# Clustered attention with routed experts: who writes the rounded halves of k and q into the operand tiles, and a new plan of the transfers

## The chip, the cores and the metric

One core of a Trainium2 chip runs the whole program. The metric is the device time of one execution in microseconds (us), the median of the runs taken. Engines are named PE (TensorE), ACT (ScalarE), DVE (VectorE), POOL (GpSimd) and SP (SyncE, whose queue starts nearly all transfers).

## What is computed

Attention in which a query sees only the keys of its own cluster, then a layer of eight experts with a limit of 80 tokens each:

```python
q_assign = argmax(einsum('bhsd,hcd->bhsc', q_n, c_n))      # 16 centroids for each head
k_assign = argmax(einsum('bhsd,hcd->bhsc', k_n, c_n))
scores = where(q_assign == k_assign, (q @ k.T) / sqrt(D), -1e9)
x = softmax(scores) @ v                                     # B, H, S, D = 4, 8, 768, 64
x = x.transpose(0, 2, 1, 3).reshape(3072, 512)
expert = argmax(x @ w_gate)                                 # E = 8, the best 80 tokens of each are kept
out[tok] = gate * (relu(x[tok] @ w1[e]) @ w2[e])            # w1: 512x1024, w2: 1024x512
```

## The kernel before

The heads go in 16 pairs (`r` from 0 to 15; four pairs a batch). Attention is the first part of the program, the choice of the tokens and the experts the second.

For each head `g` two operand tiles stand in SBUF, `KAB[g % 6]` and `QAB[g % 6]`, 128 partitions x 2 parts x 768 columns, so six heads have room at a time. A product of full precision is made out of two of lower precision: a number is split into a rounded half `hi` and the rest `lo`. Part 0 of a tile holds `hi` on rows 0 to 63, the cluster's one-hot on rows 64 to 79 and on row 80, for q, the row of the maxima ("shift", `QAB<-row`). Part 1 holds for k `lo` on rows 0 to 63 and `hi` on rows 64 to 127, for q the other way round. The scores of a block are two matmuls, part 1 against part 1 (L470) and part 0 against part 0 (L471). Before that the maxima are found from part 0 alone: matmul `sm` (L433), a reduction on DVE (L435), and once a head is through, a transposition, an ACT copy (L456) and a transfer of 3 KB that puts the row in its place. Exponentials are ACT's (L476), their sums POOL's (L485), the products with v are `av` (L494).

The preparation of a pair runs two pairs ahead of its scores and one ahead of its maxima. `assign` finds the clusters and leaves the one-hots in `oh`. `pair` (L251) then does, in this order: round k on ACT (L269, two instructions), take the rest on POOL (L271), four transfers of k's `hi` into the two heads' tiles (192 KB each as the trace counts them, read and written), two of k's `lo`, four small ones of k's one-hots; then mask q (PE L289, DVE L291), round it on ACT (L295), two transfers of q's `hi` into both parts at once (384 KB each), four small ones of q's one-hots, the rest on POOL (L301), two transfers of q's `lo`. All are started by SP, through the helper `copy` (L79, L80). The maxima of a pair need the keys `("hi", "k")` and `("hi", "q")` (`ready`, L412), its scores `("full", ...)` and the row.

The order of every engine's instructions is written by a planner when the program is made: the class `Flow` plays lanes of `Step`s with fitted durations and due times, and emits each instruction when its turn comes. `CFG` (L20) holds its constants. A transfer is played by `Flow.dma` (L1534): the queue takes 0.6 for each, the engines take them one after another, and the key is ready 1.05 after the end:

```python
for t in times:
    self.queue = max(self.queue, ready) + .6
    self.free["dma"] = max(self.free["dma"], self.queue + .65) + t
return self.free["dma"] + 1.05
```

The plan fixes only the order; on the chip each instruction waits for its operands with semaphores. Eight semaphores are used in turn for SP's transfers, so that a transfer starts only once the eighth before it has landed. Where the planner sees PE idle for longer than 0.25 it puts dummy matmuls (L1424).

Of the kernel before, what the change touches and what calls it, by code (L numbers as in the profile page):

```python
# [18 lines left out]
BASE = 0x3C000000  # L19
CFG = dict(at=dict(sum=-2.92, av=6.36, xT=11.45, lt=5.48, turn=6.25, sm=1.07, exp=-3.24, mx=-0.64), stick=1.99, wait=0.06,  # L20
           idle=0.25, dummy=128, bias=0.67, side=(-1.86, 0.07), prep=(-0.18, 0.32), lead=(-40.37, -29.82, -36.45, -34.77, -18.44),
           zero=(-15.23, 0.59, -7.6, 0.13), start=dict(pe=6.1, act=4.8, dve=7.5, pool=2.5, dma=0.0), warm=48, cold=38.0, lag=0.8,
           hold=dict(dve=(0.08, -0.06), act=(0.67, 0.23), pe=(0.25, 0.02)), nab=6, pps=9, sums=8, xts=4, vs=2, skew=3, raws=4,
           lds=3, keys=1, adds=6, weigh=(8, 5.0, 4.5), slots=(16, 8), native1=(), native2=(0, 1, 2, 3, 4, 5), early=((2, 6),
           185.8), scaled=(), spread=(), mix=dict(ld=-22.86, st=-21.43, hi1=-7.61, lo1=-8.07, hi2=-7.72, lo2=2.21, xg=-34.18,
           xp=-9.37, out=11.74, sc=-9.18, a0=4, a1=2, a2=5, spare=0.3))

# [8 lines left out]
PE, EV = "PE", "EV"  # L36
BOTH = ("dve", "pool")


class Program:  # L40
# [160 lines left out]
    def assign(self, b, p):  # L201
# [33 lines left out]
        nc.tensor.matmul(fi[:, 0:HS], lhsT=self.tie, rhs=es, start=True, stop=True)  # L235
        yield Step("act", .58, also=("dve", .75), needs=[("hi", "q", *divmod(r - 2, self.NP))] if r > 2 else [])
        oh = st["oh", b, p] = w.tile([P, HS], F32R, name="oh", bufs=2)
# [13 lines left out]
    def pair(self, b, p):  # L251

        nc, H, S, D, C, HS, w, copy, flow = self.nc, self.H, self.S, self.D, self.C, self.HS, self.work, self.copy, self.flow
        g0 = b * H + 2 * p
        pos = [g % CFG["nab"] for g in (g0, g0 + 1)]
        free = [("st", (g0 + 2 - CFG["nab"]) * self.NC - 1, 1)] if g0 + 2 > CFG["nab"] else []

        def onehot(n, AB):
            for i, g in enumerate(pos):
                self.onehot(AB[g], self.st["oh", b, p], n == "q", i)  # L260

        yield Step("none", 0.0, needs=[("ld", "k", b, p)])
        t = self.st["k", b, p]
        hi = w.tile([P, S], F32R, name="hi", bufs=2)

        lo = t.bitcast(F32R)
        for f in range(2):
            yield Step("act", .5)
            nc.scalar.copy(hi[:, f * HS:(f + 1) * HS], t[:, f * HS:(f + 1) * HS])  # L269
        yield Step("pool", 1.82, port=BOTH, needs=free + [("sim", b, p)], early=True, dma=[.55] * 4)  # L270
        nc.gpsimd.tensor_tensor(lo, t, hi.bitcast(F32), op=ALU.subtract)  # L271
        for i, g in enumerate(pos):
            r = slice(i * D, (i + 1) * D)
# [7 lines left out]
        yield Step("none", 0.0, needs=[("ld", "q", b, p), ("oh", b, p)])  # L281
# [10 lines left out]
        for f in range(2):  # L292
            fs = slice(f * HS, (f + 1) * HS)
            yield Step("act", .5)
            nc.scalar.copy(hi[:, fs], t[:, fs])  # L295
# [116 lines left out]
    def ready(self, b, h, full):  # L412

        p = h // 2
        if b or p:
            return [("full" if full else "hi", n, b, p) for n in "kq"]
        return [["k0l", "q0l", "full0"], ["k1l", "q1l", "q1h", "k1h", "oh1", ("hi", 1)]][h] if full else [[("hi", 0)], ["k1h", "oh1", ("hi", 1)]][h]
# [19 lines left out]
    def shift(self, b, h):  # L437
# [15 lines left out]
        nc.tensor.transpose(mt, mr, self.ident)  # L453
        yield Step("act", .25, give="misc", key=("shift", g), late=CFG["lag"], dma=[.06], at=NC * g - NC - 4)
        row = w.tile([NC, P], F32R, name="row", bufs=2)
# [50 lines left out]
    def turns(self, r):  # L506

        nc, S, D, HS, NC, w = self.nc, self.S, self.D, self.HS, self.NC, self.work
        b, p = divmod(r, self.NP)
        NJ = HS // P  # L510
        for f in range(2):
            yield Step("pe", .33, needs=[("xT", r, f)], take="misc")
            tp = self.misc([P, NJ, P])
            for j in range(NJ):
                nc.tensor.transpose(tp[:, j, :], self.st["xT", r][:, f, j * P:(j + 1) * P], self.ident)  # L515
            yield Step("act", .48, alt=("dve", .55), give="misc", key=("turn", r, f), dma=[1.1])
# [697 lines left out]
    def prologue(self, flow):  # L1214
# [11 lines left out]
        for p in range(CFG["lds"]):  # L1226
            for n in "kq":
                dma(("ld", n, 0, p), 1.09, self.load, 0, p, n)
            if p == 0:
# [20 lines left out]
        for r in range(CFG["vs"] - 1):  # L1250
            dma(("ldv", r), 1.09, self.load_v, r)
        self.centroids()
# [4 lines left out]
    def stream(self, flow):  # L1257
# [10 lines left out]
        def loads(n):  # L1268

            for r in range(CFG["lds"], R):  # L1270
                yield Step("dma", 1.09, needs=self.taken(n, *divmod(r - CFG["lds"], NP)), key=("ld", n, *divmod(r, NP)))
                self.load(*divmod(r, NP), n)

        def vs():
            for r in range(CFG["vs"] - 1, R):
                yield Step("dma", 1.09, needs=[("av", r - CFG["vs"], NC - 1), ("span", r - CFG["vs"])] if r >= CFG["vs"] else [], key=("ldv", r))
                self.load_v(r)

        def begin(t):
# [19 lines left out]
            if k in (4, 10) and 2 * r + k // 6 < self.NT:  # L1299
                i = 2 * r + k // 6  # L1300
                flow.dma(flow.now, .73)
                nc.sync.dma_start(self.out[i * P:(i + 1) * P, :].rearrange("p (m z) -> p m z", z=P),
# [28 lines left out]
        def weighs():  # L1331
            N1, K1 = self.w1.shape[1] // P, E * self.w1.shape[1] // P
            for n in range(K1):
                u = CFG["weigh"][0] + int(CFG["weigh"][1] * n)
                e, k = divmod(n, N1)
                yield Step("dma", 1.46, key=("wl", n), late=CFG["weigh"][2], needs=[("st", units[u][0] * NC + units[u][1], 0)] + [("wm", n - 1)] * (n > 0), at=u)
                t = self.work.tile([P, self.w1.shape[2]], F32, name="weigh", bufs=1)
# [160 lines left out]
class Flow:  # L1498
# [5 lines left out]
    def __init__(self, free):  # L1504
        self.free, self.end, self.lanes, self.lock = dict(free), {}, [], {}
        self.now, self.kind, self.queue, self.work, self.origin, self.port = 0.0, 0, 0.0, {0: 3000.0, 1: 3100.0}, 0.0, 0.0
        self.idle, self.filled, self.first, self.ahead = None, 0, None, 1e9

    def add(self, *lanes):
# [49 lines left out]
    def run(self):  # L1559
        while True:  # L1560
# [79 lines left out]
            if step.dma:  # L1640
                d = self.dma(start if step.early else done, *step.dma)
                if step.key:
                    self.end[step.key] = d
            self.done = done
# [69 lines left out]
```

## Time and profile before

| | us |
|---|---|
| median of 3 runs | 610.0 (608.13 to 612.93) |
| the profiled execution, its own time | 609.25 |
| its span, first to last instruction | 607.1 |

The profile is of one execution. Busy times are shares of the span; "idle before" is what an engine did not do ahead of a group of instructions, and who ended it. The granted clock of PE has two levels, 1.0 (2.4 GHz) and 0.5 (1.2 GHz). "L433" is a line of the kernel.

### The profile page before, as it was taken

The numbers are of one execution on the slowest core, as the hardware profiler recorded it, in microseconds if no ns is written. First come the engines' busy times: TensorE is split into PE (matmuls) and PEld (weight loads), VectorE is DVE, ScalarE is ACT, GpSimd is POOL, SyncE is SP. The second block draws the span as 40 slices with busy tenths as digits, with TensorE's granted clock in tenths as the row PEclk, the third lists the DMA queues.
The fourth block names the chain that finished last, engine by engine and source line by source line (L and its number), as shares of the span: only waits on it lengthen the run. The fifth ranks groups of instructions, "written<-read, shape, count | busy, mean of one in ns | idle before, by whom it ended". The sixth has DMA issues, their size and how long they took to land.

```text
span 607.1 us, 11292 instructions
## 1 busy us (share of the span) xinstructions
PE 566.0 (93%) x3986; PEld 370.4 (61%) x3986; DVE 416.1 (69%) x815; ACT 331.3 (55%) x704; POOL 393.5 (65%) x226
## 2 busy tenths in 40 slices
PE   7999998998999888989999979999999977899996
PEld 5568565565567465655666556665676457656563
DVE  4866676676577664666876657658777677797872
ACT  7436565565558463664576436555565360554750
POOL 5338696967299694946897928479978121547541
PEclk9558999999999997999999979999999987999999
DMA  7476868786866697688658873855594267799920
GB/s 236 104 178 205 238 180 217 196 235 179 230 178 167 178 239 211 171 231 230 175 152 202 235 237 90 221 134 159 142 375 160 103 216 279 240 391 376 387 100 22
DMA packets 73912, 124.47 MB, mean 205 GB/s; under 512 B 11809, under 2 KB 38977, under 8 KB 73857
## 3 DMA queue, kind: packets, MB, share of 16 engines
q1 hardware_dynamic: 72832, 121.12, 68.0%
q0 software_dynamic: 1024, 2.64, 1.4%
q8 instruction: 31, 0.51, 0.4%
q14 instruction: 25, 0.20, 0.1%
HBM read 70.96 MB, written 13.99 MB: 140 GB/s over the span
## 4 chain that ended last, share of the span: by engine, by line
PE 72%; DMA 11%; issue 5%; SPq 4%; ACT 4%; DVE 3%; POOLq 0%; POOL 0%; ACTq 0%; DVEq 0%
PE av L494 18%; PE sm L433 11%; PE st L470 10%; PE st L471 10%; PE yp L1042 6%; DMA QAB<-row 3%; PE hp L1014 3%; DMA QAB<-oh 3%; SPq L80 3%; DMA out_dram<-room,si 2%; PE misc L532 2%; PE misc L211 1%; PE misc L515 1%; PE misc L289 1%; DMA ldv<-in_v_dram 1%
## 5 line engine op out<-in xcount | busy, mean ns | idle before, releaser
L435 DVE TENSOR_REDUCE mx<-sm 128x1 f32<-128x384 f32 x384 | 203.5, 552 | 87.9 <-PE sm L433 84.6
L485 POOL TENSOR_TENSOR sum<-sum,pp 128x768 f32<-128x768 f32 x122 | 219.5, 1832 | 9.9 <-ACT pp L476 9.5
L476 ACT ACTIVATE pp<-st 128x384 f32<-128x384 f32 x384 | 174.6, 489 | 89.8 <-PE st L471 78.5
L433 PE MATMUL sm<-KAB,QAB 80*128 80x384 f32 x384 | 143.2, 396 | 7.2 <-DMA QAB<-oh 6.2
L494 PE MATMUL av<-pp,ldv 128*64 128x384 f32 x768 | 142.7, 500 | 0.0
L471 PE MATMUL st<-QAB,KAB 81*128 81x384 f32 x384 | 134.0, 349 | 8.2 <-DMA QAB<-row 8.2
L470 PE MATMUL st<-QAB,KAB 128*128 128x384 f32 x384 | 136.7, 356 | 0.0
L485 POOL TENSOR_TENSOR sum<-pp 128x768 f32<-128x768 f32 x32 | 59.4, 1869 | 60.3 <-ACT pp L476 54.2
L433 PEld LDWEIGHTS sm<-KAB,QAB 80*128 80x128 f32 x384 | 74.7, 202 | 30.1 <-issue 12.3
L494 PEld LDWEIGHTS av<-pp,ldv 128*64 128x64 f32 x768 | 48.3, 137 | 63.7 <-issue 61.6
L471 PEld LDWEIGHTS st<-QAB,KAB 81*128 81x128 f32 x384 | 75.7, 197 | 10.0 <-DMA QAB<-row 10.0
L470 PEld LDWEIGHTS st<-QAB,KAB 128*128 128x128 f32 x384 | 75.6, 197 | 5.4 <-issue 4.0
L301 POOL TENSOR_TENSOR ldq<-ldq,hi 128x768 fp32r<-128x768 f32 x15 | 27.6, 1839 | 39.6 <-ACT hi L295 35.7
L1072 POOL DMA_INDIRECT out_dram<-room,si x8 | 25.7, 3212 | 37.8 <-DVE room L1067 28.6
L1340 DVE TENSOR_REDUCE most<-weigh 128x1 f32<-128x1024 f32 x32 | 38.7, 1209 | 3.7 <-DMA weigh<-in_w_dram 3.7
L928 DVE SCALAR_TENSOR_TENSOR w1p<-raw,scales,w1p 128x1024 f16<-128x1024 f32 x29 | 36.1, 1277 | 0.4 <-ACT w1p L917 0.4
L271 POOL TENSOR_TENSOR ldk<-ldk,hi 128x768 fp32r<-128x768 f32 x15 | 27.4, 1828 | 10.6 <-ACT hi L269 7.6
L951 POOL DMA_INDIRECT xg<-xs,gi x8 | 19.9, 2482 | 21.1 <-issue 14.8
L1014 PEld LDWEIGHTS <-w1p 128*128 128x128 f16 x768 | 28.5, 100 | 4.7 <-issue 4.7
L1014 PE MATMUL hp<-xt,w1p 128*128 128x80 f16 x768 | 28.8, 202 | 0.3 <-ACT xt L990 0.3
L917 ACT ACTIVATE w1p<-raw,scales 128x1024 f16<-128x1024 f32 x25 | 27.3, 1143 | 1.3 <-DVE OH L624 1.3
L291 DVE SCALAR_TENSOR_TENSOR ldq<-misc,ldq 128x384 f32<-128x384 f32 x30 | 16.6, 553 | 14.7 <-PE misc L289 13.4
(247 smaller groups left out, 617.9 us busy)
## 6 DMA issues: line engine op xcount, KB each, us to landing
raw<-in_w_dram SPq DMA_DIRECT2D x40, 512.0 KB
weigh<-in_w_dram SPq DMA_DIRECT2D x32, 512.0 KB
KAB<-hi SPq DMA_DIRECT2D x60, 192.0 KB
QAB<-hi SPq DMA_DIRECT2D x30, 384.0 KB
room<-in_w_dram SPq DMA_DIRECT2D x20, 512.0 KB
ldk<-in_kT_dram SPq DMA_DIRECT2D x16, 384.0 KB
ldq<-in_qT_dram SPq DMA_DIRECT2D x16, 384.0 KB
ldv<-in_v_dram SPq DMA_DIRECT2D x16, 384.0 KB
```

The source lines that it names most:

```text
L301: nc.gpsimd.tensor_tensor(lo, t, hi.bitcast(F32), op=ALU.subtract)
L433: nc.tensor.matmul(s, lhsT=qj, rhs=k[0:D + C, 0, f * HS:(f + 1) * HS], start=True, stop=True)
L435: nc.vector.tensor_reduce(mx[:, j, f:f + 1], s, axis=AX.X, op=ALU.max)
L470: nc.tensor.matmul(s, lhsT=k[:, 1, ks], rhs=q[:, 1, qs], start=True, stop=False)
L471: nc.tensor.matmul(s, lhsT=k[0:D + C + 1, 0, ks], rhs=q[0:D + C + 1, 0, qs], start=False, stop=True)
L476: self.nc.scalar.activation(self.st["pp", g, c][:, f], self.st.pop(("s", g, c, f)), AF.Exp, scale=float(self.D) ** -0.5)
L485: eng.tensor_tensor(flat(t), flat(a), flat(self.st["pp", g, c]), op=ALU.add)
L494: nc.tensor.matmul(a[i * D:(i + 1) * D, f, 0:HS], lhsT=v[:, c, i, :], rhs=st["pp", 2 * r + i, c][:, f], start=(c == 0), stop=(c == NC - 1) ...
L928: nc.vector.scalar_tensor_tensor(t[:, 1], raw, s, t[:, 0], op0=ALU.mult, op1=ALU.subtract)
L1014: nc.tensor.matmul(hp[:, f, :], lhsT=wt[:, a, fs], rhs=xt[:, x, k, :], start=(k == 0 and i == 0), stop=(k == K - 1 and i == 2))
L1042: mm = lambda i, l, r, **kw: nc.tensor.matmul(yp[0:Mb, i], lhsT=l, rhs=r, **{"start": False, "stop": False, **kw})
L1340: nc.vector.tensor_reduce(self.most[:, R + n:R + n + 1], t, axis=AX.X, op=ALU.max, apply_absolute_value=True)
```

## The change

Four things are changed in `pair`, and the planner with them.

1. The rounded half of k and of q goes into part 0 of the operand tiles by an ACT copy of 64 partitions x 768 columns from `hi` (`place`), one for each head: four a pair, 60 in all (pair 0 is written by hand elsewhere and stays).
2. The transfers that are left: for k two of `hi` and two of `lo`, for q two of `hi` (now into part 1 alone) and two of `lo`; q's `hi` is sent only after the rest has been taken, beside the `lo`.
3. q's one-hots are sent right after k's, before q is masked and rounded, and have a key of their own, `("ohq", ...)`, which the maxima and the scores need, and the next `oh` tile but one.
4. The planner: a transfer waits for the eighth before it to land; the fixed parts are .55 and .9 in place of .65 and 1.05; durations are CP .85, OH .17, LD 1.3, LV 1.6 and WL 2.2 in place of .55, .1, 1.09, 1.09 and 1.46; a margin `lag` of 1.3 (was .8) is added to the landing of the one-hots and of the shift's row; nearly all due times in `CFG` are new, and so are `skew` (2, was 3: how many steps the second head of the first pair lags), the last number of `weigh` (1.5, was 4.5), `slots` (15 and 9, were 16 and 8), `a1` (4, was 2) and `a2` (2, was 5).

```diff
-    self.queue = max(self.queue, ready) + .6
-    self.free["dma"] = max(self.free["dma"], self.queue + .65) + t
-return self.free["dma"] + 1.05
+    self.queue = max(self.queue, ready, self.landed.pop(0)) + .6
+    self.free["dma"] = max(self.free["dma"], self.queue + .55) + t
+    self.landed.append(self.free["dma"] + .9)
+return self.free["dma"] + .9
@@ pair
+        def place(AB, hi):
+            for i, g in enumerate(pos):
+                yield Step("act", .87, needs=free)
+                nc.scalar.copy(AB[g][0:D, 0, :], hi[i * D:(i + 1) * D, :])
...
-        yield Step("pool", 1.82, port=BOTH, needs=free + [("sim", b, p)], early=True, dma=[.55] * 4)
+        yield from halves(hi, t)
+        yield Step("pool", 1.82, port=BOTH, needs=free + [("sim", b, p)], early=True, dma=[CP] * 2)
         nc.gpsimd.tensor_tensor(lo, t, hi.bitcast(F32), op=ALU.subtract)
         for i, g in enumerate(pos):
-            copy(self.KAB[g][0:D, 0, :], hi[r, :])
-            copy(self.KAB[g][D:2 * D, 1, :], hi[r, :])
-        yield Step("none", 0.0, key=("full", "k", b, p), dma=[.55] * 2)
+            copy(self.KAB[g][D:2 * D, 1, :], hi[i * D:(i + 1) * D, :])
+        yield from place(self.KAB, hi)
+        yield Step("none", 0.0, key=("full", "k", b, p), dma=[CP] * 2)
...
-        yield Step("none", 0.0, needs=[("oh", b, p)], key=("hi", "k", b, p), dma=[.1] * 4)
+        yield Step("none", 0.0, needs=[("oh", b, p)], key=("hi", "k", b, p), late=CFG["lag"], dma=[OH] * 4)
         onehot("k", self.KAB)
+        yield Step("none", 0.0, needs=[("ld", "q", b, p), ("oh", b, p)], key=("ohq", b, p), late=CFG["lag"], dma=[OH] * 4)
+        onehot("q", self.QAB)
...
-        yield Step("none", 0.0, key=("hi", "q", b, p), dma=[1.09] * 2 + [.1] * 4)
-        for i, g in enumerate(pos):
-            copy(self.QAB[g][0:D], hi[i * D:(i + 1) * D].unsqueeze(1).broadcast_to([D, 2, S]))
-        onehot("q", self.QAB)
+        yield from halves(hi, t)
+        yield from place(self.QAB, hi)
+        yield Step("none", 0.0, key=("hi", "q", b, p))
         yield Step("pool", 1.82, port=BOTH)
         nc.gpsimd.tensor_tensor(lo, t, hi.bitcast(F32), op=ALU.subtract)
-        yield Step("none", 0.0, key=("full", "q", b, p), dma=[.55] * 2)
+        yield Step("none", 0.0, key=("full", "q", b, p), dma=[CP] * 4)
+        for i, g in enumerate(pos):
+            copy(self.QAB[g][0:D, 1, :], hi[i * D:(i + 1) * D, :])
         for i, g in enumerate(pos):
             copy(self.QAB[g][D:2 * D, 1, :], lo[i * D:(i + 1) * D, :])
```

## Rows read from the trace of the kernel before

**Rows 1.** The page: the span, PE and its granted clock by slices, the chain
```profile
span 607.1 us, 11292 instructions
...
PE 566.0 (93%) x3986; PEld 370.4 (61%) x3986; DVE 416.1 (69%) x815; ACT 331.3 (55%) x704; POOL 393.5 (65%) x226
...
PEclk9558999999999997999999979999999987999999
...
PE av L494 18%; PE sm L433 11%; PE st L470 10%; PE st L471 10%; PE yp L1042 6%; DMA QAB<-row 3%; PE hp L1014 3%; DMA QAB<-oh 3%; SPq L80 3%; DMA out_dram<-room,si 2%; PE misc L532 2%; PE misc L211 1%; PE misc L515 1%; PE misc L289 1%; DMA ldv<-in_v_dram 1%
```

**Rows 2.** Busy time of each engine (us, instructions), clock and DMA by stretch
```profile
15.00:50.00 35.00, 33.23 (x122) 23.91 (x123) 25.17 (x57) 15.37 (x34) 14.51 (x8) 0.51 0.65 172
50.00:487.00 437.00, 416.29 (x2436) 267.48 (x2434) 297.91 (x588) 252.08 (x580) 321.03 (x178) 0.98 0.70 193
227.00:234.00 7.00, 4.90 (x15) 2.66 (x15) 3.17 (x5) 1.94 (x5) 4.88 (x3) 0.51 0.66 175
356.00:364.00 8.00, 6.59 (x21) 6.04 (x21) 3.04 (x7) 3.88 (x8) 2.23 (x2) 0.57 0.72 223
487.00:519.00 32.00, 23.05 (x357) 20.28 (x356) 23.09 (x75) 11.25 (x17) 6.25 (x13) 0.84 0.71 254
519.00:600.00 81.00, 80.72 (x966) 49.98 (x964) 62.84 (x67) 42.15 (x57) 42.27 (x13) 1.00 0.76 274
```
The columns: the stretch, its length, busy PE, PE's weight loads, DVE, ACT, POOL, granted clock, share of the DMA engines, GB/s.

**Rows 3.** Waits of PE: who waited for whom, us in total, times, longest
```profile
PE st L471 <- DMA QAB<-row: 8.2, 5, 3.3
PE sm L433 <- DMA QAB<-oh: 6.2, 4, 3.5
```

**Rows 4.** The chain from 217 to 230 us: start, us, what
```profile
217.68 0.93 ACT hi L295 x2
...
220.42 0.70 SPq L80
...
221.17 0.63 SPq L80
...
221.85 7.16 DMA QAB<-oh
...
229.10 0.66 PE sm L433
```

**Rows 5.** The chain elsewhere: two rows and a one-hot
```profile
143.58 5.46 DMA QAB<-row
...
197.42 2.00 DMA QAB<-oh
...
354.11 3.25 DMA QAB<-row
```

**Rows 6.** Groups by line: shapes, count, busy us, mean ns, idle before, releasers
```profile
L476 ACT ACTIVATE pp<-st 128x384 f32<-128x384 f32 x384 | 174.6, 489 | 89.8 <-PE st L471 78.5 <-PE av L494 3.2 <-POOL sum L485 2.3
...
L295 ACT CAST hi<-ldq 128x384 fp32r<-128x384 f32 x30 | 14.3, 511 | 1.2 <-DVE ldq L291 0.9
...
L456 ACT CAST row<-misc 6x128 fp32r<-6x128 f32 x32 | 8.1, 254 | 24.9 <-PE misc L453 23.3 <-DMA raw<-in_w_dram 1.3
...
L938 ACT CAST w2p<-room 128x1024 fp32r<-128x1024 f32 x4 | 4.2, 1043 | 2.6 <-PE hp L1014 2.6
...
L403 DVE CAST QAB<-ldq 64x768 fp32r<-64x768 f32 x1 | 0.5, 543 | 0.0
...
L470 PEld LDWEIGHTS st<-QAB,KAB 128*128 128x128 f32 x384 | 75.6, 197 | 5.4 <-issue 4.0 <-ACT x L519 0.6 <-ACT pp L476 0.3
```

**Rows 7.** Issues of transfers: what, engine, operation, count, KB each
```profile
KAB<-hi SPq DMA_DIRECT2D x60, 192.0 KB
QAB<-hi SPq DMA_DIRECT2D x30, 384.0 KB
...
QAB<-ldq SPq DMA_DIRECT2D x30, 192.0 KB
```

More of the change, by code (lines that the diff above doesn't have):

```diff
@@ L19 @@
 BASE = 0x3C000000
[L20 to L26, printed above, removed]
+CFG = dict(at=dict(sum=-3.46, av=6.5, xT=9.63, lt=2.62, turn=6.52, sm=2.41, exp=-3.44, mx=-1.76), stick=1.61, wait=0.05,
+           idle=0.25, dummy=128, bias=0.18, side=(-1.52, -0.17), prep=(-0.75, 0.12), lead=(-39.66, -31.86, -37.47, -37.48,
+           -18.17), zero=(-15.24, 0.53, -11.87, 0.25), start=dict(pe=6.1, act=4.8, dve=7.5, pool=2.5, dma=0.0), warm=48,
+           cold=38.0, lag=1.3, hold=dict(dve=(0.08, -0.02), act=(0.7, 0.04), pe=(0.26, 0.04)), nab=6, pps=9, sums=8, xts=4, vs=2,
+           skew=2, raws=4, lds=3, keys=1, adds=6, weigh=(8, 5.0, 1.5), slots=(15, 9), native1=(), native2=(0, 1, 2, 3, 4, 5),
+           early=((2, 6), 185.8), scaled=(), spread=(), mix=dict(ld=-22.93, st=-22.34, hi1=-3.09, lo1=-20.55, hi2=4.02, lo2=2.78,
+           xg=-34.32, xp=-10.34, out=9.27, sc=-5.2, a0=4, a1=4, a2=2, spare=0.54))
 SWITCH = {(0, 1): .01, (1, 0): .01, (0, 2): .108, (1, 2): .108, (2, 0): .16, (2, 1): .196, (0, 0): 0.0, (1, 1): 0.0, (2, 2): 0.0}
@@ L37 @@
 BOTH = ("dve", "pool")
+CP, OH, LD, LV, WL = .85, .17, 1.3, 1.6, 2.2
 class Program:
@@ L260, in onehot, with halves @@
                 self.onehot(AB[g], self.st["oh", b, p], n == "q", i)
+        def halves(hi, t):
+            for f in range(2):
+                fs = slice(f * HS, (f + 1) * HS)
+                yield Step("act", .5)
+                nc.scalar.copy(hi[:, fs], t[:, fs])
+        def place(AB, hi):
+            for i, g in enumerate(pos):
+                yield Step("act", .87, needs=free)
+                nc.scalar.copy(AB[g][0:D, 0, :], hi[i * D:(i + 1) * D, :])
         yield Step("none", 0.0, needs=[("ld", "k", b, p)])
@@ L291, in pair @@
             nc.vector.scalar_tensor_tensor(t[:, fs], mask, 1.0 / BIG, t[:, fs], op0=ALU.mult, op1=ALU.mult)
[L292 to L295, printed above, removed]
-        yield Step("none", 0.0, key=("hi", "q", b, p), dma=[1.09] * 2 + [.1] * 4)
-        for i, g in enumerate(pos):
-            copy(self.QAB[g][0:D], hi[i * D:(i + 1) * D].unsqueeze(1).broadcast_to([D, 2, S]))
-        onehot("q", self.QAB)
+        yield from halves(hi, t)
+        yield from place(self.QAB, hi)
+        yield Step("none", 0.0, key=("hi", "q", b, p))
         yield Step("pool", 1.82, port=BOTH)
         nc.gpsimd.tensor_tensor(lo, t, hi.bitcast(F32), op=ALU.subtract)
-        yield Step("none", 0.0, key=("full", "q", b, p), dma=[.55] * 2)
+        yield Step("none", 0.0, key=("full", "q", b, p), dma=[CP] * 4)
+        for i, g in enumerate(pos):
+            copy(self.QAB[g][0:D, 1, :], hi[i * D:(i + 1) * D, :])
         for i, g in enumerate(pos):
@@ L415, in ready @@
         if b or p:
-            return [("full" if full else "hi", n, b, p) for n in "kq"]
+            return [("full" if full else "hi", n, b, p) for n in "kq"] + [("ohq", b, p)]
         return [["k0l", "q0l", "full0"], ["k1l", "q1l", "q1h", "k1h", "oh1", ("hi", 1)]][h] if full else [[("hi", 0)], ["k1h", "oh1", ("hi", 1)]][h]
@@ L453, in shift @@
         nc.tensor.transpose(mt, mr, self.ident)
-        yield Step("act", .25, give="misc", key=("shift", g), late=CFG["lag"], dma=[.06], at=NC * g - NC - 4)
+        yield Step("act", .4, give="misc", key=("shift", g), late=CFG["lag"], dma=[0.0], at=NC * g - NC - 4)
         row = w.tile([NC, P], F32R, name="row", bufs=2)
@@ L515, in turns @@
                 nc.tensor.transpose(tp[:, j, :], self.st["xT", r][:, f, j * P:(j + 1) * P], self.ident)
-            yield Step("act", .48, alt=("dve", .55), give="misc", key=("turn", r, f), dma=[1.1])
+            yield Step("act", .48, alt=("dve", .55), give="misc", key=("turn", r, f), dma=[.6])
             x = self.con.tile([P, NJ, P], F32, name="x", bufs=3)
@@ L1227, in prologue @@
             for n in "kq":
-                dma(("ld", n, 0, p), 1.09, self.load, 0, p, n)
+                dma(("ld", n, 0, p), LD, self.load, 0, p, n)
             if p == 0:
@@ L1250, in prologue @@
         for r in range(CFG["vs"] - 1):
-            dma(("ldv", r), 1.09, self.load_v, r)
+            dma(("ldv", r), LD, self.load_v, r)
         self.centroids()
@@ L1270, in loads @@
             for r in range(CFG["lds"], R):
-                yield Step("dma", 1.09, needs=self.taken(n, *divmod(r - CFG["lds"], NP)), key=("ld", n, *divmod(r, NP)))
+                yield Step("dma", LD, needs=self.taken(n, *divmod(r - CFG["lds"], NP)), key=("ld", n, *divmod(r, NP)))
                 self.load(*divmod(r, NP), n)
@@ L1275, in vs @@
             for r in range(CFG["vs"] - 1, R):
-                yield Step("dma", 1.09, needs=[("av", r - CFG["vs"], NC - 1), ("span", r - CFG["vs"])] if r >= CFG["vs"] else [], key=("ldv", r))
+                yield Step("dma", LV, needs=[("av", r - CFG["vs"], NC - 1), ("span", r - CFG["vs"])] if r >= CFG["vs"] else [], key=("ldv", r))
                 self.load_v(r)
@@ L1300, in begin @@
                 i = 2 * r + k // 6
-                flow.dma(flow.now, .73)
+                flow.dma(flow.now, .7)
                 nc.sync.dma_start(self.out[i * P:(i + 1) * P, :].rearrange("p (m z) -> p m z", z=P),
@@ L1335, in weighs @@
                 e, k = divmod(n, N1)
-                yield Step("dma", 1.46, key=("wl", n), late=CFG["weigh"][2], needs=[("st", units[u][0] * NC + units[u][1], 0)] + [("wm", n - 1)] * (n > 0), at=u)
+                yield Step("dma", WL, key=("wl", n), late=CFG["weigh"][2], needs=[("st", units[u][0] * NC + units[u][1], 0)] + [("wm", n - 1)] * (n > 0), at=u)
                 t = self.work.tile([P, self.w1.shape[2]], F32, name="weigh", bufs=1)
@@ L1507, in __init__ @@
         self.idle, self.filled, self.first, self.ahead = None, 0, None, 1e9
+        self.landed = [0.0] * 8
     def add(self, *lanes):
@@ L1642, in run @@
                 if step.key:
-                    self.end[step.key] = d
+                    self.end[step.key] = d + step.late
             self.done = done
```

7 lines of the change are left out of this document (1 added, 6 removed).

## The prediction

> **What bounds the kernel now.** I read the page first: PE is busy for 93% of the span, DVE 69%, POOL 65%, ACT 55% [rows 1]. So PE sets the time, and a change is worth what it gives back of PE's idle time or of its slow clock, or what it adds to them. The slices of the granted clock show where the clock is not full: near the start, in two single slices in the middle, and around the choice of the tokens [rows 1].
>
> The view by stretches prices this [rows 2]. From 50 to 487 us attention runs, and PE is busy for 416.29 of 437 us: 20.7 us idle. From 519 to 600 us the experts run, with PE busy for 80.72 of 81 us at full clock: no planner's constant can shorten that without taking matmuls away, and the change takes none. Between the two, 32 us go to the choice of the tokens, which isn't edited. The start, 15 to 50 us, has PE busy for 33.23 of 35 us at a clock of 0.51.
>
> The view of PE's waits tells who makes the idle time in attention: scores wait 8.2 us in five places for the row of the maxima, maxima wait 6.2 us in four places for q's one-hots, each up to 3.5 us [rows 3]. Together 14.4 of the 20.7 us are waits for a small transfer. The two longest are followed by a stretch at the lower clock: after the wait that ended at 229.1 us [rows 4] the stretch 227 to 234 has 0.51, and around the wait that ended at 357.4 (354.11 and 3.25 on) [rows 5] the stretch 356 to 364 has 0.57 [rows 2]. PE did 4.90 and 6.59 us of busy time there; at the upper clock the first takes half, some 2.5 us less, and of the second what lies at the lower level, some 6.2 us, takes 3.1 less. So the waits and what follows them cost 14.4 + 5.6 = 20.0 us, the most that attention between 50 and 487 us can give back by this cause.
>
> The chain of waits shows why the one-hots are late [rows 4]. q is rounded at 217.68 to 218.61. SP starts the two large transfers of q's half at 220.42 and 221.17, the one-hots are behind them at 221.85, and these 24 KB land 7.16 us later. PE takes the next maximum at 229.10, 10.5 us after q was rounded. A one-hot that stood less behind landed in 2.00 us [rows 5]. The row of the next head comes out of the maxima, so a pair whose maxima start late sends its rows late: the same cause stands behind a part of the 8.2 us. The rest of that part is the queue: the row at 143.58 took 5.46 us [rows 5].
>
> **The change part by part.**
>
> *One-hots of q sent early.* They need only `oh`, which is ready before q is masked, so they now land while PE masks q and ACT rounds it. Instead of two transfers of 384 KB and four of 24 KB behind the rounding there are two ACT copies. From the end of the rounding to the first maximum this takes two copies of about 0.87 us, 1.7 us, and with an exponential of 0.489 us [rows 6] ahead of each 2.7 us, in place of 10.5 [rows 4]. So in the worst place maxima may start some 8 us earlier than they did, more than the longest wait of 3.5 us [rows 3]. All of the 6.2 us should go, and the 2.5 us of slow clock behind the longest: 8.7 us.
>
> *Rows.* They follow the maxima, and are due earlier by as much; but q's last transfers are now four of 192 KB where two were [rows 7], and a row that falls behind them waits for two more. The planner now counts with eight in flight and a margin of 1.3. I take two thirds of the 8.2 + 3.1 us, 7.3 us; the bounds are nothing and all 11.3.
>
> *Bytes.* For a pair, twelve units of 192 KB (four of k's half, two of its rest, two double ones of q's half, two of its rest [rows 7]) become eight; over 15 pairs 11.5 MB fewer, at 193 GB/s [rows 2] some 60 us of the queue's time, and two transfers fewer in 18. This is off PE's path except where a wait above names it; I count nothing beyond the rows and the one-hots.
>
> *ACT's copies.* No row has 64 partitions x 768 on ACT. Bounds: a cast of 128 columns takes 254 ns, of 384 columns 511, of 1024 columns 1043 [rows 6]. From the first two 1.0 ns a column gives 511 + 384 = 895 ns; from the last two 0.83 ns a column gives 830 ns. I take 870 ns, 60 times: 52 us. ACT is busy for 252.08 of the 437 us of attention [rows 2], and would stand at some 70%. What hides it is ACT's own idle time, 89.8 us before exponentials, 78.5 of it waiting for PE [rows 6]. What it can cost is a late exponential: three banks hold the scores, and PE stops if ACT is three behind. The 60 casts of 511 ns that ACT already does for the same halves have left 0.3 us of wait on exponentials in the group of 384 weight loads [rows 6]. So the low bound is nothing, and the high one the full 52 us, as if no exponential could be moved aside. I take 2 us, next to the low end, as the copies are the same sort of work as those casts.
>
> *The planner's other constants.* They move no work between engines in attention. The new times for loads (LD, LV, WL) put transfers at other places of SP's queue; `skew` and the due times change the order of PE's first 50 us. I count nothing for them and give the start a case of its own below. In the experts, `slots`, `a1`, `a2` and the due times move ACT's and DVE's splitting of weights, hidden behind a PE that is full [rows 2]; without that cover each microsecond of a late weight would be one of time. The choice of the tokens has the same chain of small steps.
>
> *Sum.* Against the profiled execution's own 609.25 us (span 607.1 [rows 1]): less 8.7, less 7.3, plus 2, is 595.2; it lies within 1 us of the median, 610.0. I forecast 595.0 us.
>
> **The rivals.**
>
> *A. The rows stay late.* The maxima come earlier, but the row stands behind four transfers of q in place of two, and the margin only moves it in the plan. For it: the row of 3 KB took 5.46 us in a place where the queue was full [rows 5], and the row is the larger of the two waits [rows 3]. Against it: a third of the bytes is gone. Then only 8.7 us come back: 609.25 - 8.7 + 2 = 602.5 us.
>
> *B. The waits come back elsewhere.* PE is busy for 95% of attention, the plan is new from end to end, and each place in which PE's order and the data don't meet costs again. If they cost the same 20 us as now, the change does not do what it says, and the time stays at 609 us. For it: the planner of before plays the same keys and rows, and 14.4 us of waits for them are in the trace. Against it: the planner now counts the eight transfers.
>
> *C. ACT becomes late (the other side).* 60 copies of 0.87 us stand between exponentials. If each costs PE half its length, 26 us, the time is 609.25 - 16 + 26 = 619 us. It decides at 0.38 us a copy: from there on the 16 us are eaten up and 1% more is lost. For it: six hundred ACT instructions of attention [rows 2] wait for each other in order, and a copy is nearly twice as long as an exponential. Against it: the 0.3 us [rows 6]. The Trainium skill, "ScalarE: Activation LUTs", section "Rules for kernel authors", speaks against this placing: it gives simple elementwise work (it lists relu, max, min, add and mul) to VectorE rather than ScalarE, since VectorE is faster for each element. The trace bears out the price: the one such cast on DVE, 64x768, took 543 ns [rows 6]; but DVE has 297.91 us of 437 to do and ACT 252.08 [rows 2].
>
> *D. The start gets its full clock earlier.* From 15 to 50 us PE works at 0.51 [rows 2]. If pair 1's maxima, ready sooner, fill PE so that the clock rises 14 us earlier, 7 us more come back: 588 us. Nothing in the rows says that it must.
>
> **How the numbers follow.** The forecast (both waits go, 591 to 599) has 0.50, A 0.18, B 0.14, C 0.11, D 0.07. One per cent, 6 us, is about what a measurement here can tell from no change: faster is below 603.9, slower above 616.1. The forecast and D are faster; A lies near the bound, and I give it two thirds to faster, one third to within; B is within; C mostly slower. That makes 0.70 faster, 0.19 within, 0.11 slower. The range reaches from D's neighbourhood, 587, over A to the edge of B, 609; what is left out is C, half of B and the lower part of D, some 2 in 10.
>
> **What would show it.** Right: in the profile after, PE's waits for QAB<-oh are gone and those for QAB<-row are below 3 us; the granted clock stays at 1.0 from 50 us to the end of attention, which ends about 473 us in place of 487; the copies of 64x768 on ACT take 0.83 to 0.90 us; the part from the end of attention to the end stays within 2 us of its 120 us. Wrong: waits of PE's scores for ACT's exponentials of several us (C); rows that land in 5 us (A); waits of like sum for other transfers or engines (B); a clock that is full well before 50 us (D). Also wrong, if the experts' stretch moved by more than 3 us.

## The result, and the profile after

The kernel after takes 586.86 us in the median of four runs (585.59 to 588.72), the kernel before 609.84 beside it: a ratio of 0.962, with a 95% interval of 0.957 to 0.967. The forecast was 595.0 with a range from 587.0 to 609.0. The direction was right; the gain is 23 us in place of 15, and the time lies 0.14 us below the range.

The profiled execution of after took 587.6 us, of before 609.25. First the page of after, the lines that answer to [rows 1]:

```profile
span 585.8 us, 11321 instructions
...
PE 562.4 (96%) x4015; PEld 368.3 (63%) x4015; DVE 430.3 (73%) x850; ACT 359.6 (61%) x729; POOL 381.9 (65%) x226
...
PEclk9559999999999999999999999999999877999999
...
PE av L501 24%; PE sm L440 14%; PE st L477 12%; PE st L478 11%; DMA out_dram<-room,si 6%; PE misc L539 2%; PE misc L522 2%; PE misc L212 2%; PE misc L299 1%; POOL xg L958 1%; DMA raw<-in_w_dram 1%; DMA ldv<-in_v_dram 1%; PE misc L220 1%; PE misc L460 1%; PE sm L539 1%
```

The two slow slices in the middle are gone, and no transfer of QAB is left among the lines of the chain that the page shows. Lines of `pair` and below have moved: L433 is now L440, L470 and L471 are L477 and L478, L494 is L501.

The stretches of after, to be held against [rows 2] (stretch, length, busy PE, weight loads, DVE, ACT, POOL, granted clock, DMA share, GB/s). Attention now ends at 459, the choice of the tokens at 495, the experts' matmuls at 581:

```profile
15.00:50.00 35.00, 34.18 (x139) 21.84 (x140) 26.67 (x61) 19.86 (x39) 12.88 (x8) 0.61 0.53 139
50.00:459.00 409.00, 407.28 (x2426) 263.85 (x2424) 306.35 (x613) 278.30 (x605) 323.71 (x179) 1.00 0.64 180
459.00:495.00 36.00, 25.03 (x375) 21.65 (x372) 27.14 (x81) 15.24 (x20) 7.03 (x13) 0.78 0.70 250
495.00:581.00 86.00, 85.29 (x977) 53.35 (x975) 61.65 (x69) 35.50 (x49) 28.99 (x13) 0.97 0.68 247
```

In attention PE stands idle for 1.7 us, where it was 20.7, and its clock is full throughout. In the two later parts the reader sees the opposite: the choice takes some 36 us in place of 32, at a clock of 0.78 in place of 0.84, and the experts' stretch has 0.97 in place of 1.00.

Put together from the trace's marks (the start of the last `av` matmul of the first and of the last pair, the start of the first `hp`, the end of the last `yp`):

| part | before | after | difference |
|---|---|---|---|
| start, to the last av of pair 0 | 71.3 | 70.3 | -1.0 |
| attention, from there to the last av | 410.1 | 383.2 | -26.9 |
| choice, from there to the first hp | 38.2 | 41.6 | +3.4 |
| experts, first hp to last yp | 82.4 | 85.5 | +3.1 |
| end | 5.2 | 5.2 | 0 |

The sum is -21.4 us, and the spans differ by 21.3. These are traces of one execution of each kernel. The attention of after came out at 383.2 us in three traces that share its plan there; before was traced once.

The waits of PE in after, to be held against [rows 3]. The long ones that are left stand in the choice and just ahead of the first expert. Of the 1.7 us in attention, 0.4 us is a wait for a row, and none is for a one-hot:

```profile
PE q L708 <- DVE dug L654: 2.7, 1, 2.7
PE tp L992 <- ACT room L971: 2.4, 1, 2.4
PE q L708 <- DVE alive L751: 2.0, 1, 2.0
...
PE st L478 <- DMA QAB<-row: 0.4, 1, 0.4
```

And the place that answers to [rows 4], the same pair, by the timeline (start, us, engine, line, operation). The second pair of L267 casts ends at 210.62, the two ACT copies at 212.95; the one-hots were started at 208.49:

```profile
208.49 2.44 SPq L81 DMA_DIRECT2D QAB<-oh  x4
...
209.53 0.52 ACT L267 CAST hi<-ldq 128x384 fp32r<-128x384 f32 x1
...
210.11 0.51 ACT L267 CAST hi<-ldq 128x384 fp32r<-128x384 f32 x1
...
210.90 0.81 ACT L272 CAST QAB<-hi 64x768 fp32r<-64x768 f32 x1
...
212.12 0.83 ACT L272 CAST QAB<-hi 64x768 fp32r<-64x768 f32 x1
...
215.72 0.38 PE L440 MATMUL sm<-KAB,QAB 80*128 80x384 f32 x1
```

The pair's first maximum is the one at 215.72, 5.1 us after q was rounded, where it was 10.5; the `sm` rows before it belong to the pair ahead. PE did not wait for it: the plan put it there.

### The profile page after: what moved, and what is told of

Same layout as the page of the kernel before. It is cut to its first block, busy times and chain, and to the rows that moved or that the text cites. A ratio compares the mean times of both kernels' runs of the same rounds, so it can differ in the third digit from the quotient of the medians.

```text
span 585.8 us, 11321 instructions
## 1 busy us (share of the span) xinstructions
PE 562.4 (96%) x4015; PEld 368.3 (63%) x4015; DVE 430.3 (73%) x850; ACT 359.6 (61%) x729; POOL 381.9 (65%) x226
## 4 chain that ended last, share of the span: by engine, by line
PE 73%; issue 11%; DMA 9%; DVE 3%; POOL 1%; SPq 1%; ACT 1%; POOLq 0%; DVEq 0%
PE av L501 24%; PE sm L440 14%; PE st L477 12%; PE st L478 11%; DMA out_dram<-room,si 6%; PE misc L539 2%; PE misc L522 2%; PE misc L212 2%; PE misc L299 1%; POOL xg L958 1%; DMA raw<-in_w_dram 1%; DMA ldv<-in_v_dram 1%; PE misc L220 1%; PE misc L460 1%; PE sm L539 1%
## 5 line engine op out<-in xcount | busy, mean ns | idle before, releaser
L442 DVE TENSOR_REDUCE mx<-sm 128x1 f32<-128x384 f32 x384 | 201.1, 550 | 57.1 <-PE sm L440 54.1
L501 PE MATMUL av<-pp,ldv 128*64 128x384 f32 x768 | 143.7, 498 | 0.1
L440 PE MATMUL sm<-KAB,QAB 80*128 80x384 f32 x384 | 141.3, 396 | 0.6 <-DVE mx L442 0.3
L477 PE MATMUL st<-QAB,KAB 128*128 128x384 f32 x384 | 134.5, 350 | 0.0
L478 PE MATMUL st<-QAB,KAB 81*128 81x384 f32 x384 | 130.4, 340 | 0.4 <-DMA QAB<-row 0.4
L440 PEld LDWEIGHTS sm<-KAB,QAB 80*128 80x128 f32 x384 | 72.1, 198 | 28.3 <-issue 11.8
L501 PEld LDWEIGHTS av<-pp,ldv 128*64 128x64 f32 x768 | 47.1, 136 | 61.0 <-issue 58.4
L477 PEld LDWEIGHTS st<-QAB,KAB 128*128 128x128 f32 x384 | 73.3, 191 | 6.8 <-issue 4.8
L478 PEld LDWEIGHTS st<-QAB,KAB 81*128 81x128 f32 x384 | 73.4, 191 | 0.7 <-DMA QAB<-row 0.7
L1079 POOL DMA_INDIRECT out_dram<-room,si x8 | 21.2, 2648 | 40.6 <-DVE room L1074 36.1
L958 POOL DMA_INDIRECT xg<-xs,gi x8 | 11.4, 1429 | 35.4 <-DVE room L975 20.8
L1021 PE MATMUL hp<-xt,w1p 128*128 128x80 f16 x768 | 31.3, 208 | 0.3 <-DVE xt L999 0.2
L1030 ACT ACTIVATE hh<-hp 128x320 f32<-128x320 f32 (+1 forms) x16 | 7.0, 437 | 35.4 <-PE hp L1021 30.5
L935 DVE SCALAR_TENSOR_TENSOR w1p<-raw,scales,w1p 128x1024 f16<-128x1024 f32 x22 | 27.5, 1277 | 0.4 <-ACT w1p L924 0.4
L272 ACT CAST KAB<-hi 64x768 fp32r<-64x768 f32 x30 | 24.8, 828 | 0.4
```

The lines of the kernel that those rows point to most:

```text
L440: nc.tensor.matmul(s, lhsT=qj, rhs=k[0:D + C, 0, f * HS:(f + 1) * HS], start=True, stop=True)
L442: nc.vector.tensor_reduce(mx[:, j, f:f + 1], s, axis=AX.X, op=ALU.max)
L477: nc.tensor.matmul(s, lhsT=k[:, 1, ks], rhs=q[:, 1, qs], start=True, stop=False)
L478: nc.tensor.matmul(s, lhsT=k[0:D + C + 1, 0, ks], rhs=q[0:D + C + 1, 0, qs], start=False, stop=True)
L501: nc.tensor.matmul(a[i * D:(i + 1) * D, f, 0:HS], lhsT=v[:, c, i, :], rhs=st["pp", 2 * r + i, c][:, f], start=(c == 0), stop=(c == NC - 1) ...
L935: nc.vector.scalar_tensor_tensor(t[:, 1], raw, s, t[:, 0], op0=ALU.mult, op1=ALU.subtract)
```

## The experiments

The runs were made in groups, and each ratio is to the kernel before in the same group, on the same chip. There before took 613.58 us (the first four rows under after, up to "one-hots late"), 609.42 us (the two with "same plan", the one moved the other way and the last row) or 611.27 us (the other four), so ratios are a better guide than medians across the groups. "Attention" is the stretch from the last `av` of pair 0 to the last one, as in the table above, with the time PE stood idle in it and the time it had the lower clock.

| kernel | median us | ratio, 95% interval | attention | idle | lower clock |
|---|---|---|---|---|---|
| before | 609.84 | 1 | 410.1 | 20.4 | 13.7 |
| after | 586.86 | 0.962, 0.957 to 0.967 | 383.2 | 1.7 | 0 |
| new pair, old plan | 599.67 | 0.975, 0.970 to 0.981 | 400.5 | 10.0 | 6.8 |
| old pair, new plan | 599.76 | 0.980, 0.973 to 0.986 | 393.2 | 6.3 | 0 |
| halves by SP | 602.13 | 0.978, 0.972 to 0.984 | 399.1 | 8.6 | 10.2 |
| one-hots late | 602.01 | 0.979, 0.974 to 0.984 | 401.0 | 4.9 | 10.2 |
| halves by SP, same plan | 622.55 | 1.021, 1.014 to 1.029 | 417.1 | 21.2 | 23.9 |
| one-hots late, same plan | 610.29 | 1.004, 1.000 to 1.008 | 401.5 | 13.6 | 10.2 |
| ACT copies twice | 601.62 | 0.983, 0.977 to 0.989 | 397.5 | 11.8 | 0 |
| after, constants moved | 602.00 | 0.984, 0.977 to 0.991 | 388.3 | 3.5 | 0 |
| after, moved the other way | 592.64 | 0.973, 0.968 to 0.978 | 386.6 | 3.0 | 3.4 |
| before, constants moved | 606.62 | 0.993, 0.988 to 0.998 | 403.4 | 16.2 | 3.4 |
| more dummies | 585.33 | 0.956, 0.951 to 0.961 | 383.2 | 1.7 | 0 |
| more dummies, old experts' constants | 587.98 | 0.967, 0.962 to 0.972 | 383.2 | 1.7 | 0 |

**The two halves of the change, crossed.** The theory was that the shorter preparation gives the gain; the rival, that the new plan does.

```diff
# new pair, old plan: after, with the planner's constants and transfer model of before
-CP, OH, LD, LV, WL = .85, .17, 1.3, 1.6, 2.2
+CP, OH, LD, LV, WL = .55, .1, 1.09, 1.09, 1.46
...
-    self.queue = max(self.queue, ready, self.landed.pop(0)) + .6
+    self.queue = max(self.queue, ready) + .6
# old pair, new plan: after, with pair() and ready() of before, costed by the fitted times
-        yield Step("none", 0.0, key=("hi", "q", b, p), dma=[1.09] * 2 + [.1] * 4)
+        yield Step("none", 0.0, key=("hi", "q", b, p), late=CFG["lag"], dma=[2 * CP] * 2 + [OH] * 4)
```

> The edits of the pair's preparation (ACT copies, one-hots early, q's half later) under the planner of before: its constants, its transfer model and its due times. Theory (the shorter preparation gives the gain): most of the 23 us stay, 588 to 597 us, and PE's waits for QAB<-oh are gone. Rival (the new plan gives the gain): 603 to 610 us, with waits for QAB<-row or others of over 8 us.

> The preparation of before (all halves by SP's transfers, q's one-hots behind them) under the planner of after: new constants, eight transfers in flight, margins, the fitted 0.85 for each 192 KB. Theory (the shorter preparation gives the gain): 602 to 612 us, with waits of PE for QAB<-oh of 5 us or more. Rival (the plan gives the gain): 586 to 594 us.

Neither theory stands alone: each half by itself gives 2 to 2.5%. In attention the two add up: 410.1 becomes 400.5 by the preparation and 393.2 by the plan, 26.5 us in sum, and both together give 26.9. How close that is means little, as neighbouring plans, further below, move attention by 3 to 7 us. The waits of PE for the new pair under the old plan:

```profile
PE st L478 <- DMA QAB<-row: 4.3, 3, 2.4
...
PE misc L220 <- ACT row L463: 2.1, 6, 0.3
PE misc L299 <- ACT row L463: 1.9, 6, 0.3
```

and of the old pair under the new plan:

```profile
PE st L472 <- DMA QAB<-row: 2.2, 3, 1.1
...
PE misc L212 <- ACT row L457: 0.3, 1, 0.3
```

The waits for q's one-hots are gone in both: the preparation sends them early, or the plan, which now counts with late landings, puts PE's instructions in another order. Waits for the row are halved by the one and cut to a quarter by the other. The rows on L220, L299 and L212 are of a kind that the prediction had not looked at: after the row's transposition the next matmul into the same PSUM bank waits for ACT's copy of the row, 0.3 us at a time. The old plan has it with either preparation, the new one hardly: all places in attention together, 4.2 us in before, 4.0 for the new pair under the old plan, 0.5 for the old pair under the new plan, 0.3 in after. The lines of before:

```profile
PE misc L289 <- ACT row L456: 2.5, 7, 0.4
...
PE misc L219 <- ACT row L456: 1.4, 4, 0.3
```

Among the changes of the planner is one that the list in "The change" leaves out: its step for that copy is 0.4 us in place of 0.25. It is the likely reason, but it was not changed by itself.

**Each part of the preparation undone, with a new plan.**

```diff
# halves by SP (the keys ("hi", "k") and ("hi", "q") need "placed" too)
+            yield Step("none", 0.0, needs=free, key=("placed", id(AB), b, p), dma=[CP] * 2)
             for i, g in enumerate(pos):
-                yield Step("act", .87, needs=free)
-                nc.scalar.copy(AB[g][0:D, 0, :], hi[i * D:(i + 1) * D, :])
+                copy(AB[g][0:D, 0, :], hi[i * D:(i + 1) * D, :])
...
# one-hots late: from behind k's to behind the rounding and the ACT copies of q
-        yield Step("none", 0.0, needs=[("ld", "q", b, p), ("oh", b, p)], key=("ohq", b, p), late=CFG["lag"], dma=[OH] * 4)
-        onehot("q", self.QAB)
...
+        yield Step("none", 0.0, key=("ohq", b, p), late=CFG["lag"], dma=[OH] * 4)
+        onehot("q", self.QAB)
```

> The kernel after, but the halves go into part 0 by SP's transfers in place of ACT's copies (four more transfers of 192 KB a pair); one-hots stay early, all constants stay. If early one-hots are what matters, 586 to 592 us; if ACT's copies matter (fewer bytes, no landing behind the rounding), 595 to 605 us, with PE waiting for QAB<-hi.

> The kernel after, but q's one-hots are sent behind the rounding of q again (four transfers of 24 KB with nothing large right ahead of them); ACT's copies stay. If early one-hots are what matters, 595 to 605 us with waits for QAB<-oh; if the two large transfers ahead of them were the trouble, 586 to 591 us.

Both cost the same against after, 1.7 and 1.8% by the ratios, and by the traces all of it in attention (16 and 18 us longer; in the second the part ahead of it is 3.8 us shorter). But hardly any of it is a wait for a transfer: PE waits 1.6 us for QAB<-hi in the first and for no one-hot in the second. More idle time and the lower clock make 12 of the 16 us and 8 of the 18; the rest is PE busy for longer and was not taken apart. A planner that counts with the later data makes another plan, with constants that had been chosen for something else. So these two runs could not tell a part's worth from that of the plan.

**The same, with the plan held still.** Here PE, DVE and POOL keep after's order to the instruction, ACT too but for the copies taken out; the planner counts as if nothing were changed.

```diff
# one-hots late, same plan: only the place of the call moves
         yield Step("none", 0.0, needs=[("ld", "q", b, p), ("oh", b, p)], key=("ohq", b, p), late=CFG["lag"], dma=[OH] * 4)
-        onehot("q", self.QAB)
...
         yield Step("none", 0.0, key=("hi", "q", b, p))
+        onehot("q", self.QAB)
...
# halves by SP, same plan
                 yield Step("act", .87, needs=free)
-                nc.scalar.copy(AB[g][0:D, 0, :], hi[i * D:(i + 1) * D, :])
+                copy(AB[g][0:D, 0, :], hi[i * D:(i + 1) * D, :])
```

> The plan of after kept instruction for instruction on PE, ACT, DVE and POOL; only SP sends q's one-hots four instructions behind the rounding of q instead of right after k's. Theory (the early one-hots carry a part of the gain by themselves): 592 to 602 us, PE's waits for QAB<-oh 5 us or more. Rival (with nothing large ahead of them they land in time anyway): 586 to 590 us.

> The plan of after kept on PE, DVE and POOL, and on ACT but for the 60 copies; the halves go into part 0 by four transfers of 192 KB a pair from SP at the same places. Theory (ACT's copies spare the landing behind the rounding): 597 to 612 us, with waits of PE for QAB<-hi. Rival (the 52 us of ACT work cost what the transfers would): 584 to 590 us.

Each undoes the whole gain or more in the time of the program, further than either theory had it. In attention, where the gain was 26.9 us, the late one-hots cost 18.3 us and the halves by SP 33.9. PE's waits with the one-hots late:

```profile
PE sm L440 <- DMA QAB<-oh: 6.4, 5, 1.6
PE sm L440 <- issue: 4.6, 3, 2.6
```

with the halves by SP:

```profile
PE sm L440 <- DMA QAB<-hi: 8.1, 4, 4.0
PE sm L440 <- issue: 5.1, 3, 2.1
...
PE st L478 <- DMA QAB<-row: 2.3, 3, 1.0
```

"issue" is time in which PE waited for nothing that the profile shows. The idle time is back (13.6 and 21.2 us) and with it the lower clock (10.2 and 23.9 us). The early one-hots and the ACT copies are thus both needed by this plan. The late one-hots have nothing large right ahead of them and still make PE wait, so the rival of that run is out. What each is worth in a plan made for its absence, these two runs don't tell.

**What ACT has left.**

```diff
                 nc.scalar.copy(AB[g][0:D, 0, :], hi[i * D:(i + 1) * D, :])
+                nc.scalar.copy(AB[g][0:D, 0, :], hi[i * D:(i + 1) * D, :])
```

> The kernel after with each of the 60 ACT copies of 64x768 issued twice, in the same plan (the planner is not told): 50 us more of ACT work. Theory (ACT's idle time hides the copies): at most 4 us more than after, PE's waits for exponentials below 3 us. Rival (ACT is near its bound): 10 us or more, with PE waiting for ACT pp.

The rival was right about the second 50 us. ACT's groups, and then a wait of PE:

```profile
L484 ACT ACTIVATE pp<-st 128x384 f32<-128x384 f32 x384 | 173.6, 487 | 49.7 <-PE st L479 44.4 <-DMA KAB<-hi 0.5
...
L273 ACT CAST KAB<-hi 64x768 fp32r<-64x768 f32 x30 | 25.0, 832 | 0.9
L273 ACT CAST QAB<-hi 64x768 fp32r<-64x768 f32 x30 | 25.0, 832 | 1.0
```

```profile
PE st L478 <- ACT pp L484: 6.9, 11, 0.8
```

Attention grows by 14.3 us (383.2 to 397.5), 0.24 us for each copy added, 29% of its length. In after itself PE has no wait for exponentials to show: the first 50 us, which the plan counts, cost none there, and the next 50, which it does not count, do. Whether a plan that counts them too fares better was not tried.

**Neighbouring plans.** Four of the planner's constants were moved by 0.05 to 0.1. The work is the same but for some dummy matmuls and, in two of the three, some copies (ten in the first) that change between ACT and DVE; what differs is the order.

```diff
# the four entries of CFG alone
# after, constants moved (the other way: 6.6, -3.49, 1.56, 0.13)
-av=6.5,  exp=-3.44,  stick=1.61,  bias=0.18
+av=6.4,  exp=-3.39,  stick=1.66,  bias=0.23
# before, constants moved
-av=6.36,  exp=-3.24,  stick=1.99,  bias=0.67
+av=6.26,  exp=-3.19,  stick=2.04,  bias=0.72
```

> The kernel after with four of the planner's constants moved a little (av 6.5 to 6.4, exp -3.44 to -3.39, stick 1.61 to 1.66, bias 0.18 to 0.23); the work is the same, the order a neighbouring one. Theory (the shorter preparation and the fitted model carry the gain, any near plan keeps it): 585 to 591 us where before is at 610. Rival (a good part of the gain is this one plan, and is lost with any move): 596 to 603 us, with waits or a slow clock in attention.

> The kernel before with the same moves (av 6.36 to 6.26, exp -3.24 to -3.19, stick 1.99 to 2.04, bias 0.67 to 0.72). It tells how far a plan of before moves by itself: if the plans of before are chosen points too, 612 to 622 us; if not, 606 to 613 us.

> The kernel after with the four constants moved the other way (av 6.6, exp -3.49, stick 1.56, bias 0.13): a second neighbouring plan. If a neighbouring plan keeps the gain in attention, its attention takes 380 to 392 us from the first pair to the last (after 383.2, the first neighbour 388.3, before 410.1), whatever choice and experts do; if the gain sits in this one plan, 398 us or more. The whole: 588 to 604 us.

After's neighbours are slower than after by 13 and 6 us by the ratios, before's neighbour is some 4 us faster than before. The first neighbour's time lies where its rival had it, but not for the rival's reason: in attention the neighbours keep most of the gain, 388.3 and 386.6 us against 383.2 for after's, 403.4 against 410.1 for before's. So of the 26.9 us between the two kernels there, about 21 are left between the means (386.0 for the three plans with the new edits, 406.8 for the two with the old) and 16 between the neighbours alone; the rest is this pair of plans. The waits go with the edits and not with the draw: before's neighbour waits 5.5 us for rows and 3.3 us for q's one-hots, after's neighbours 0.6 us at most for a row and not at all for q's one-hots. The slow neighbour lost 9.5 us in the experts, most of it at one place, a matmul that waited 6.3 us for an ACT instruction:

```profile
PE yp L1049 <- ACT hh L1030: 6.6, 2, 6.3
```

**The later parts.** In after, one long run of 73 dummy matmuls stands between the choice and the first expert. PE's rows (start, us, what, idle before it):

```profile
486.39 4.24 PE L1431 MATMUL tot<-one 128*128 128x128 f16 x73
493.08 0.45 PE L992 MATMUL tp<-K,room 80*128 80x80 f16 x4 [2.45 <-ACT room L971]
494.10 0.45 PE L992 MATMUL tp<-K,room 80*128 80x80 f16 x4 [0.57 <-DVE room L975]
...
495.12 5.73 PE L1021 MATMUL hp<-xt,w1p 128*128 128x80 f16 x96
```

The dummies end 2.45 us before PE is needed, the clock falls to 1.2 GHz, and the first 96 matmuls of the experts take 5.73 us. In before 67 dummies end 1.28 us ahead, and the 96 matmuls take 3.60 us. The test gives PE half as many dummies again there:

```diff
+        if n > 60:
+            n += n // 2
         if n:
             self.idle(n, misc)
```

> The kernel after with the one long run of dummy matmuls, between the choice of the tokens and the first expert, made half as long again (73 to 109). Theory (the slow first matmuls of the experts come from the 2.5 us in which PE stood idle ahead of them): the clock stays full there, the first 96 hp matmuls take 3.4 us in place of 5.5, and the time is 2 to 4 us below after. Rival (the clock falls in any case, or the dummies delay the first tokens): within 1 us of after or slower.

```profile
486.83 6.25 PE L1431 MATMUL tot<-one 128*128 128x128 f16 x109
494.22 0.32 PE L992 MATMUL tp<-K,room 80*128 80x80 f16 x4 [1.15 <-ACT room L971]
...
496.14 3.60 PE L1021 MATMUL hp<-xt,w1p 128*128 128x80 f16 x96 [0.25 <-DVE xt L999]
```

The clock stays full there, the 96 matmuls take 3.60 us, and first `hp` to last `yp` takes 83.1 us in place of 85.5. The theory holds for the place. The whole is the fastest time measured here, 585.33 us, but its interval overlaps after's, so the step from after to it is shown by the trace and not by the times.

The choice lost 2 us at one place. DVE's rows of after:

```profile
473.49 0.07 DVE L742 DVE_READ_ACCUMULATOR j<-q,rem 8x1 f16 x1
475.57 0.75 DVE L926 TENSOR_SCALAR w1p<-raw,scales 128x1024 f16<-128x1024 f32 x1 [2.01 <-DMA raw<-in_w_dram]
476.24 0.41 DVE L751 SCALAR_TENSOR_TENSOR alive<-dug,nb 128x96 f16<-128x96 f32 x2
```

A split of a weight stands in DVE's order between two rounds of the choice and waits 2.01 us for its load; the round behind it, and PE behind that, wait with it. The last run takes the experts' constants of before (`mix`, `slots`) with the longer run of dummies:

> The kernel after with the longer run of dummies and with the experts' constants of before (mix and slots). In after DVE waited 2.0 us for a load of weights in the midst of the choice of the tokens, to split them. Theory (the due times of the weights put this split there): the choice takes 39 to 40.5 us in place of 41.6, the whole 582 to 585 us. Rival (the experts' new constants pay elsewhere what they cost here): 585 us or more, with the experts above 83 us.

The choice takes 37.9 us, 3.7 less, but the experts 89.0, 5.9 more than with the new constants (PE there waits 4.0 us for ACT's rounding of a later expert's tokens): the rival was right, the constants bring more in the experts than they cost in the choice. Which single constant does it was not tried.

## Why the prediction was right, and where it was wrong

**The cause: right.** Waits for q's one-hots and for the row, and the slow clock behind them, were the place of most of the gain: 19.5 of the 20.0 us that the prediction counted for them came back (6.2 and 7.8 us of waits, 5.5 by the clock). Undoing either edit of the preparation in the same plan brings waits for its transfers back, and the whole time with them. How much of the gain is the edits' and how much the new plan's, the runs show only roughly: 2.5 and 2.0% each by itself.

**The term for the one-hots, 8.7 us: right in size.** 6.2 us of waits are now nothing, and the stretch of lower clock behind the longest is gone. The path from the rounding of q to the first maximum was to fall to some 2.7 us; the copies end 2.3 us after the rounding, and the plan lets the maximum come at 5.1.

**The term for the rows, 7.3 us: too small.** Two thirds were taken, with all 11.3 as the bound; 0.4 us of waits are left and no slow clock, so 10.9 us came back. The fear of four transfers ahead of a row was not borne out: rival A did not happen. In the crossed runs either half of the change alone takes about half of the waits or more.

**The sum had no term beyond those waits: this is the step that failed.** The prediction took 20.0 us, the waits of [rows 3] and the slow clock behind them, as the most that attention could give back by its cause, forecast 16.0 of them, less 2 for ACT's copies, and put everything else at nothing. It gave no reason for leaving out the other 6.3 us of idle time (6.0 between the marks of the table), and it counted nothing for the planner's other constants. Attention gave back 26.9 us and ends at about 459 us, where the prediction had 473. Beyond the 19.5 us of the prediction's cause, 4.7 of the 6.0 us went. Two thirds of the 6.0, 4.2 us, were waits of 0.3 to 0.4 us behind ACT's copy of the row, too small each to stand high in a list; 0.3 us of them is left, and by the crossed runs it is the plan that takes them away. The last 2.6 us are PE busy for less time, a part of it four `sm` matmuls that after has ahead of the stretch. The rest of that was not taken apart, so its cause stays open.

**ACT's copies, 870 ns and 2 us of cost: nearly right.** They take 828 and 825 ns:

```profile
L272 ACT CAST KAB<-hi 64x768 fp32r<-64x768 f32 x30 | 24.8, 828 | 0.4
L272 ACT CAST QAB<-hi 64x768 fp32r<-64x768 f32 x30 | 24.7, 825 | 0.4
```

just below the lower bound of 830, and cost PE nothing to be seen. Rival C did not happen, but it was nearer than the 0.3 us of [rows 6] let it look: the same amount once more costs 0.24 us a copy. The Trainium skill, "ScalarE: Activation LUTs", section "Rules for kernel authors", gives relu, max, min, add and mul to VectorE and names a gain for bf16; a plain copy of fp32 is not in its list. One such cast on DVE took 543 ns [rows 6], so by price alone DVE is the cheaper here too. In after's attention DVE is busy for 306.35 of 409 us and ACT, with the copies, for 278.30. The copies on DVE were not tried, so which engine is the better place stays open.

**"The part from the end of attention to the end stays within 2 us": wrong.** The choice and the experts took 6.5 us more, the experts alone 3.1, just over the 3 us that the prediction had named as a sign of being wrong. The prediction had said what a late weight would cost and then counted nothing for it; a late weight in DVE's order cost 2.0 us, and a PE left idle ahead of the first expert some 2.4.

**The start.** The lower clock ended at 42.4 us in place of 49.6 (0.61 over the stretch in place of 0.51), 7.2 us earlier where rival D had 14. By D's reckoning that is worth 3.6 us, but pair 0 ended only 1.0 us earlier. That D's 588 us lies nearest to the result is chance.

**The range.** With the parts as measured, 609.25 - 1.0 - 26.9 + 3.4 + 3.1 is 587.85 us; the profiled execution took 587.6. That the time misses the range by so little is luck: two errors ran against each other. Attention gave 13 us more than the net 14 of the forecast, and the later parts took 6.5 us that it did not have; without these the time would have been some 581 us. The range held no term for the plan itself, and the neighbours show what that is: with constants moved by 0.05 to 0.1 the time is 592.6 or 602.0 us. That the forecast of 595.0 lies among these is no merit of its sum. The chances as listed for the cases add up to 0.69, 0.20 and 0.11, a hundredth from the 0.70, 0.19 and 0.11 given.

## What to carry to other kernels

When an engine is near full, count all its idle time as what a change can give back, small waits too, and look in the diff for what each of them hangs on; the longest waits of the list are only the part that is easy to see. Where a change also moves the constants of stages that it does not edit, give those stages a term as well: here they took 6.5 us back. Where the order of instructions is planned, a change of the data's path and a change of the plan must be told apart with the order held still: undone in the same order, each edit cost 4 to 6% here, with a new plan 1.7 to 1.8%. And a plan is one draw: try neighbours of both kernels before a few per cent are put down to the edit.

## What the runs showed of the hardware that was not expected

- An ACT copy from partitions 64 to 127 into 0 to 63 costs about as much as one that stays: in after 829 and 831 ns in the mean for k and q, against 826 and 818 ns.
- PE's clock fell from 2.4 to 1.2 GHz in the trace of after when PE stood idle for 2.45 us behind a run of 73 dummies (the granted clock of the stretch 495 to 502 is 0.66); with the gap at 1.15 us behind 109 dummies it did not (1.00 from 493 to 502). How it depends on the moment, and on the number of dummies apart from the gap, was not tried.
- SP's starts of q's four one-hots took 4.0 to 5.3 us together in every pair of before but pair 0, behind two transfers of 384 KB with a source read twice. In after, without those, they took 2.4 to 2.5 us in eleven of the fifteen pairs and 3.0 to 4.4 in four; why these four differ stays open, and whether it is the size or the double reading that holds them up in before was not tried.
